# Building the keys of the second head pair on GpSimd, and turning its queries in larger pieces, in an attention and mixture-of-experts kernel

## The chip, the core and the metric

One core of a Trainium2 chip runs the whole program. The metric is device time in microseconds (us): the median of a few executions, each from the first to the last instruction of the program and what lies around it. Smaller is better.

## What is computed

Attention with rotary position codes for 4 batches of 8 heads (576 positions, 64 numbers a head), followed by a mixture of 8 experts in which each token takes one expert:

```python
q_rot, k_rot = rotate(q), rotate(k)                  # x1*cos - x2*sin, x1*sin + x2*cos
attn = softmax(q_rot @ k_rot.T / sqrt(64))
x = attn @ v                                         # heads side by side: 4 x 576 x 512
e = expert_of_token(x)                               # argmax of gates, or the token before's
out = p[e] * (relu(x @ w1[e]) @ w2[e])
```

The output must be as good as fp32. So the kernel splits a number into a rounded part (fp32r, "hi") and the rest ("lo"), and multiplies both.

## The kernel before, in words

**Pairs and steps.** Two heads make a pair; 4 batches of 4 pairs give pairs 0 to 15. A pair takes 9 steps: for each of its two heads four tiles of 128 queries, and one tile that holds the last 64 queries of both heads. So there are 144 steps, and step g belongs to pair g // 9. In each step (the loop from L1270) TensorE computes the scores of the next step (`mm_s`, L255, L273: 4 matmuls of 288 columns; 6 or 10 in a tile of tails), VectorE takes their minimum (L278), ScalarE the exponential (L295), TensorE transposes the result of two steps before (L332), ScalarE rounds that to hi (L310), VectorE subtracts to lo (L314), and from step 11 on TensorE multiplies with the values (L371), five matmuls a step. Up to step 117 the order on every engine is the order of the program. The scores of a step lie in one of two PSUM buffers, so the scores of step g + 2 wait for the exponential of step g.

**What the scores need.** `m` holds a pair's keys: for each head, hi and lo, each on all 128 partitions (the 64 rows twice). `qst` holds its queries, hi in the upper and lo in the lower 64 partitions; `qtail0`/`qtail` hold the tails. There are two buffers for `m` and for `qst`; pair p uses number p % 2.

**Pairs 2 to 15** get them as follows. SyncE (SP) loads q and k in two forms (`load_qk`), GpSimd (POOL) multiplies both with tables of cosines and sines and adds them (`rope_k`, `rope_q`, L200 and L201), splits the sums into hi and lo (`split_qk`, L212 and L213), and SP copies the result to where it is needed with DMAs inside SBUF (`spread`): two for the tails (L240), six for the keys (`spread_k`, L227 to L229) and four for the queries (`spread_q`, L235). A score matmul waits for those copies alone that write what it reads: step 19, the first of pair 2 that is no tile of tails, reads head 0, so it waits for keys' copies one and four and for queries' copies one and three.

**Pairs 0 and 1** are made in another way, in `first_pair` (L1111), so that the work can start early. Their q and k are loaded in a form in which one table multiplication (`products`, L1140; for pair 1 on POOL) leaves two halves that only have to be added, and TensorE adds and duplicates them by a matmul with a 0/1 matrix (`turned`, L1143). ScalarE then rounds the PSUM result to hi (L1152, L1178) and VectorE computes lo (L1155, L1184). Pair 1's keys are made in four pieces of 288 columns (`half_keys`), its queries in four pieces of 256 and 320 columns (`queries`, the second piece of a head with its tail).

**What sets the order around the change.** The dict `START` (L1246) says at the end of which step each of these is issued: pair 1's pieces in steps 3 to 7; `rope_2` and `split_qk(2)`, which make pair 2's queries and keys on POOL, in step 3; `spread(2)` in step 8. POOL and SP work strictly in that order too. On POOL before step 3 stand the four multiplications for pair 1 (L1217) and `split_v(0)` (L218, L219). The loads of the start stand in SP's queue in the order of the program: pair 0's, then pair 1's four (L1201), `wid` (the identity for the transposes, L1229), pair 0's values, a table (L1231), pair 2's, another table, and others.

```python
m_t[1] = m_p.tile([P, 2, 2, S], F32R, tag="m", name="m_1")
pair_1 = [lambda a=a, h=h: half_keys(a, h) for a in range(2) for h in range(2)]
```

## Time and profile before

| | |
|---|---|
| Median of 3 runs | 537.85 us (537.2 to 539.41) |
| The profiled execution's own time | 537.79 us |
| Its span, first to last instruction | 536.0 us |
| TensorE (PE) busy | 515.5 us, 96% of the span |
| VectorE (DVE) busy | 379.1 us, 71% |
| ScalarE (ACT) busy | 344.9 us, 64% |
| GpSimd (POOL) busy | 346.0 us, 65% |
| Mean granted TensorE clock | 0.995 |

Times in the profile count from the start of the span. L12 is line 12 of the kernel. A row of the timeline merges neighbouring instructions of one kind: start, length, engine, line, operation, output<-inputs, count, and in brackets the idle time of the engine before it with what ended that. PEld is TensorE's loading of weights, which runs ahead of the matmuls (PE); DMAs are issued by SP (SPq).

### The profile page before, as it was taken

Reading aid. Unit: us, or ns where it says so; the run is one execution under the profiler, and the core shown is the slowest. Engines: PE = TensorE matmul, PEld = TensorE weight load, DVE = VectorE, ACT = ScalarE, POOL = GpSimd, SP = SyncE. Lnnn points to the kernel's source line nnn. Section 1 sums busy time; section 2 is a strip of 40 time slices with the busy share of each in tenths; the row PEclk is TensorE's granted clock in tenths of the full one; section 3 lists DMA queues with packets and bytes.
Section 4 is the critical chain, followed back from the end, with each engine's and each line's share of the span. In section 5 each row is a group of like instructions: output and inputs, shape, how many; then the busy total and the mean of one; then the engine's idle time right before and its main releaser. Section 6 shows DMA issues by size and latency. Waiting matters only on the chain.

```text
span 536.0 us, 10810 instructions
## 1 busy us (share of the span) xinstructions
PE 515.5 (96%) x3273; PEld 459.1 (86%) x3273; DVE 379.1 (71%) x690; ACT 344.9 (64%) x766; POOL 346.0 (65%) x290
## 2 busy tenths in 40 slices
PE   7999999999999999999999899999999999999992
PEld 4889999999999999998978688887888888888881
DVE  6999999999999999999998746447421745421630
ACT  3988999999999999987866423252433344533440
POOL 4999999999999999795898202355512554411332
PEclk9999999999999999999999999999999999999998
DMA  8758878987889879866168214553637486547340
GB/s 270 285 127 224 229 211 242 239 183 213 226 225 245 206 180 238 228 162 137 24 205 230 66 32 165 169 226 105 191 101 235 141 332 181 172 102 235 98 160 25
DMA packets 65481, 97.33 MB, mean 182 GB/s; under 512 B 28353, under 2 KB 39105, under 8 KB 65282
## 3 DMA queue, kind: packets, MB, share of 16 engines
q1 hardware_dynamic: 61938, 86.45, 57.3%
q0 software_dynamic: 3040, 9.71, 5.8%
q8 instruction: 28, 0.46, 0.4%
q14 instruction: 43, 0.35, 0.2%
q10 hardware_dynamic: 432, 0.36, 0.2%
HBM read 76.95 MB, written 12.86 MB: 168 GB/s over the span
## 4 chain that ended last, share of the span: by engine, by line
PE 80%; DVE 9%; issue 3%; ACT 3%; POOL 2%; DMA 1%; ACTq 0%; POOLq 0%; SPq 0%; DVEq 0%
PE h L981 18%; PE o L1024 17%; PE pv L371 14%; PE s L273 13%; PE tm L332 9%; PE gx L457 3%; DVE mn L278 2%; PE th L1015 2%; DVE ptl L314 2%; PE tx L967 1%; ACT e L295 1%; PE tk L342 1%; DVE w L926 1%; DMA turn<-in_turn_dram 1%; DMA rows_d<-xrow 1%
## 5 line engine op out<-in xcount | busy, mean ns | idle before, releaser
L1024 PE MATMUL o<-w,hs 128*128 128x512 f32 x456 | 113.0, 398 | 0.0
L278 DVE TENSOR_REDUCE mn<-s 128x1 f32<-128x576 f32 x144 | 107.1, 745 | 2.4 <-PE s L273 1.1
L981 PE MATMUL h<-w,xs 128*128 128x512 f32 x444 | 106.1, 392 | 1.2 <-DVE xs L314 0.9
L295 ACT ACTIVATE e<-s,mn 128x576 f32<-128x576 f32 x128 | 95.4, 745 | 16.4 <-DVE mn L278 13.9
L314 DVE TENSOR_TENSOR ptl<-tm,pth 128x512 fp32r<-128x512 f32 x139 | 95.5, 688 | 11.8 <-ACT pth L310 8.8
L1030 POOL DMA_INDIRECT out_dram<-os,sidx x19 | 23.3, 1229 | 124.5 <-ACTq L932 83.0
L273 PE MATMUL s<-m,qst 128*128 128x288 f32 x512 | 96.8, 311 | 4.6 <-ACT e L295 2.7
L981 PEld LDWEIGHTS h<-w,xs 128*128 128x128 f32 x444 | 82.6, 188 | 19.4 <-DVE xs L314 1.4
L1024 PEld LDWEIGHTS o<-w,hs 128*128 128x128 f32 x456 | 83.1, 188 | 17.0 <-DVE hs L314 0.4
L310 ACT CAST pth<-tm 128x512 fp32r<-128x512 f32 x139 | 80.6, 580 | 7.1 <-PE tm L332 6.5
L273 PEld LDWEIGHTS s<-m,qst 128*128 128x128 f32 x512 | 74.1, 188 | 10.1 <-ACT e L295 5.3
L332 PE MATMUL tm<-wid,e 128*128 128x128 f32 x512 | 77.0, 272 | 0.0
L371 PE MATMUL pv<-pth,v 128*128 128x288 f32 x256 | 76.7, 315 | 0.1
L371 PE MATMUL pv<-ptl,v 128*128 128x288 f32 x256 | 76.5, 314 | 0.1
L200 POOL TENSOR_TENSOR stage<-stage 128x1152 f32<-128x1152 f32 x26 | 69.3, 2666 | 0.9 <-DMA stage<-in_qk_dram 0.9
L332 PEld LDWEIGHTS tm<-wid,e 128*128 128x128 f32 x512 | 62.1, 140 | 0.8 <-DVE ptl L314 0.4
L926 DVE TENSOR_TENSOR w<-stage,w 128x1024 fp32r<-128x1024 f32 x37 | 51.2, 1420 | 14.5 <-ACT w L923 9.7
L371 PEld LDWEIGHTS pv<-pth,v 128*128 128x128 f32 x256 | 48.3, 189 | 1.4 <-issue 0.4
L371 PEld LDWEIGHTS pv<-ptl,v 128*128 128x128 f32 x256 | 48.3, 189 | 0.5 <-POOL ptl L307 0.4
L314 DVE TENSOR_TENSOR xs<-tx,xs 128x512 fp32r<-128x512 f32 x19 | 13.1, 688 | 44.1 <-ACTq L932 34.3
L201 POOL TENSOR_TENSOR stage<-stage 128x576 f32<-128x576 f32 x26 | 37.0, 1423 | 2.0
L314 DVE TENSOR_TENSOR hs<-th,hs 128x512 fp32r<-128x512 f32 x26 | 17.5, 687 | 27.4 <-ACTq L932 15.8
(202 smaller groups left out, 822.0 us busy)
## 6 DMA issues: line engine op xcount, KB each, us to landing
stage<-in_wts_dram SPq DMA_DIRECT2D x84, 512.0 KB
stage<-in_qk_dram SPq DMA_DIRECT2D x26, 576.0 KB
qst<-xq SPq DMA_DIRECT2D x56, 128.0 KB
stage<-in_v_dram SPq DMA_DIRECT2D x16, 320.0 KB
m<-xq SPq DMA_DIRECT2D x14, 288.0 KB
m<-xk SPq DMA_DIRECT2D x14, 288.0 KB
m<-xq SPq DMA_DIRECT2D x14, 256.0 KB
m<-xk SPq DMA_DIRECT2D x14, 256.0 KB
```

Source lines behind the costliest of these rows:

```text
L200: engine.tensor_tensor(x, x, tab[:, 2 * f:2 * f + 2], op=ALU.mult)
L201: engine.tensor_tensor(rr[:, f], x[:, 0], x[:, 1], op=ALU.add)
L273: pe.matmul(st[:, h, lo:hi], lhs, keys[:, k0:k0 + hi - lo], start=(n == 0), stop=(n == len(parts_) - 1))
L278: dve.tensor_reduce(mn, s_t[g][:, :, 0:HALF], axis=AX.XY, op=ALU.min)
L295: act.activation(dst.rearrange("p (h s) -> p h s", h=2), s_t.pop(g)[:, :, 0:HALF], AF.Exp, bias=mn, scale=-1.0, accum_out=sums[:, col:col ...
L310: act.copy(hi, src)
L314: dve.tensor_tensor(lo, src, hi.bitcast(F32), op=ALU.subtract)
L332: pe.transpose(ps[:, k], src[:, k * P:(k + 1) * P], ident)
L371: pe.matmul(pv_t[p, u], lhs.rearrange("p c d -> p (c d)"), rhs, start=(n == 0), stop=(n == 9))
L926: (pool if k in on_pool else dve).tensor_tensor(lo, src, hi.bitcast(F32), op=ALU.subtract)
L981: pe.matmul(ps[:, c], xs_t[t][:, x, k], w[y][:, c * 512:(c + 1) * 512], start=(k == 0 and n == 0), stop=(k == 3 and n == 2))
L1024: pe.matmul(ps, hs_t[t][:, x, k], w[y][:, (k % 2) * 512:(k % 2 + 1) * 512], start=(k == 0 and n == 0), stop=(k == 7 and n == 2))
```

## The change

Pair 1's keys are no longer made by TensorE, ScalarE and VectorE. POOL multiplies their two forms by two tables, adds them and splits them into hi and lo, and SP spreads them with the six DMAs of `spread_k(1)`, issued in step 2 ahead of `load_qk(3)`. For this they are loaded in the form of the later pairs, and the fourth table (`tab[:, 3]`) is loaded earlier, between pair 1's second and third load; pair 1's loads come in the order 0, 2, 3, 1. Pair 1's queries are turned in one piece of 512 columns a head (steps 4 and 5), and both heads' tails in a piece of 128 columns (step 7). The function that makes pair 0's remaining keys loses its arguments for pair 1.

```diff
     def split_qk(p):
         parts = [(xq, rr)] if p % 2 == 0 else [(xk[1], rr[:, 1]), (xq[:, :, 0], rr[:, 0])]
         for x, src in parts:
-            pool.tensor_scalar(x[:, 0], src, 1.0, 1.0, op0=ALU.mult, op1=ALU.mult)
-            pool.tensor_tensor(x[:, 1], src, x[:, 0].bitcast(F32), op=ALU.subtract)
+            split_half(x, src)
+
+    def split_half(x, src):
+        pool.tensor_scalar(x[:, 0], src, 1.0, 1.0, op0=ALU.mult, op1=ALU.mult)
+        pool.tensor_tensor(x[:, 1], src, x[:, 0].bitcast(F32), op=ALU.subtract)
...
         dve.memset(raw[:, 0, :, 0:1], 0.0)
-        for x in (2, 3, 0, 1):
+        for x in (0, 2, 3, 1):
+            if x == 3:
+                sp.dma_start(tab[:, 3], tabs[:, 3])
             sp.dma_start(raw[:, 0, x], qk[0, 1, :, x])
...
-        for x in (2, 3, 0, 1):
-            products(x, engine=pool, of=raw[:, 0])
-        m_t[1] = m_p.tile([P, 2, 2, S], F32R, tag="m", name="m_1")
-        pair_1 = [lambda a=a, h=h: half_keys(a, h) for a in range(2) for h in range(2)]
-        pair_1 += [lambda a=a, lo=lo, hi=hi: queries(a, lo, hi, 1)() for a in range(2) for lo, hi in ((0, 256), (256, S))]
+        products(0, engine=pool, of=raw[:, 0])
+        for x in range(2):
+            pool.tensor_tensor(raw[:, 0, 2 + x], raw[:, 0, 2 + x], tab[:, 2 + x], op=ALU.mult)
+        pool.tensor_tensor(rr[:, 1], raw[:, 0, 2], raw[:, 0, 3], op=ALU.add)
+        split_half(xk[1], rr[:, 1])
+        products(1, engine=pool, of=raw[:, 0])
+
+        def queries_1(a):
+            ps = ps_t.tile([P, 512], F32, tag="t", name=f"q1_{a}")
+            turned(a, ps, 0, 512, raw[:, 0])
+            return scaled(qst[1][:, a], ps)
+
+        def tails_1():
+            ps = ps_t.tile([P, 512], F32, tag="t", name="q1_tail")
+            for a in range(2):
+                turned(a, ps[:, 64 * a:64 * a + 64], 512, 64, raw[:, 0])
+            dst = qtail0[1].rearrange("p a (c s) -> p (a c) s", c=2)[:, 0:4:3]
+            return scaled(dst, ps[:, 0:P].rearrange("p (a s) -> p a s", a=2))
+
+        def scaled(dst, src):
+            act.activation(dst, src, AF.Copy, scale=-0.125)
+            low = slice(64, 128)
+            dve.scalar_tensor_tensor(dst[low], src[low], -0.125, dst[low].bitcast(F32), op0=ALU.mult, op1=ALU.subtract)
+
+        pair_1 = [lambda: queries_1(0), lambda: queries_1(1), tails_1]
...
-        sp.dma_start(tab[:, 3], tabs[:, 3])
...
-            0: [lambda: split_v(0)], 1: [rest_q[1], lambda: keep_awake(1)], 2: [rest_q[2], lambda: load_qk(3)],
-            3: [pair_1[0], pair_1[1], rope_2, lambda: split_qk(2)], 4: [pair_1[2]], 5: pair_1[3:5],
-            6: pair_1[5:6], 7: pair_1[6:8] + [lambda: split_v(1), lambda: load_v(2)],
+            0: [lambda: split_v(0)], 1: [rest_q[1], lambda: keep_awake(1)], 2: [rest_q[2], lambda: spread_k(1), lambda: load_qk(3)],
+            3: [rope_2, lambda: split_qk(2)], 4: pair_1[0:1], 5: pair_1[1:2],
+            7: pair_1[2:3] + [lambda: split_v(1), lambda: load_v(2)],
             8: [lambda: spread(2)], 40: [lambda: act.copy(trib, trif)],
```

## Rows read from the trace of the kernel before

**Rows 1.** The chain that ended last, by line: 13 to 30 us, then 44 to 225 us.

```profile
by line: DVE mn L278 29.2%; DVE ptl L314 16.7%; DVE qst L1184 14.6%; issue 10.4%; DVE m L1155 10.0%; ACT e L295 4.9%; DVE qtail L1184 3.4%; PE q L1144 3.2%; ACT pth L310 2.8%; ACT qst L1178 2.3%; ACT pkh L310 1.6%; PE s L273 0.8%; ACT qtail
...
by line: PE pv L371 33.0%; PE s L273 32.3%; PE tm L332 24.0%; PE gx L457 7.3%; PE tk L342 2.7%; PE tt L348 0.7%; issue 0.1%
```

**Rows 2.** Stretches: busy us (and count) of each engine, clock, DMA share, GB/s.

```profile
15.00:20.00 5.00, 4.74 (x33) 4.25 (x33) 4.88 (x10) 4.59 (x13) 4.92 (x4) 1.00 1.01 401
```

**Rows 3.** VectorE to 30 us by shape: count, busy us, mean ns, idle before.

```profile
L314 DVE TENSOR_TENSOR ptl<-tm,pth 128x512 fp32r<-128x512 f32 x8 | 5.5, 689 | 0.2
L1184 DVE SCALAR_TENSOR_TENSOR qst<-q,qst 64x256 fp32r<-64x256 f32 x8 | 3.3, 427 | 0.5 <-ACT qtail L1178 0.3
L1155 DVE TENSOR_TENSOR m<-k,m 128x288 fp32r<-128x288 f32 x6 | 2.5, 450 | 0.0
...
L1184 DVE SCALAR_TENSOR_TENSOR qtail<-q,qtail 64x64 fp32r<-64x64 f32 x4 | 0.9, 222 | 0.0
```

**Rows 4.** Timeline of TensorE: score matmuls of step 10 and loads of steps 19, 28.

```profile
27.31 0.78 PE L273 MATMUL s<-m,qst 128*128 128x288 f32 x4 [0.54 <-DVE qst L1184]
...
43.50 0.56 PEld L273 LDWEIGHTS s<-m,qst 128*128 128x128 f32 x4 [0.35 <-ACT et L295]
...
59.93 0.58 PEld L273 LDWEIGHTS s<-m,qst 128*128 128x128 f32 x4
```

**Rows 5.** Timeline of GpSimd.

```profile
9.20 1.43 POOL L1141 TENSOR_TENSOR raw<-raw,stage 128x576 f32<-128x576 f32 x1
11.10 4.14 POOL L1141 TENSOR_TENSOR raw<-raw,stage 128x576 f32<-128x576 f32 x3 [0.47 <-DMA raw<-in_qk_dram]
...
20.23 1.41 POOL L201 TENSOR_TENSOR stage<-raw 128x576 f32<-128x576 f32 x1
...
27.08 2.68 POOL L213 TENSOR_TENSOR xq<-stage,xq 128x1152 fp32r<-128x1152 f32 x1
...
40.33 0.67 POOL L212 TENSOR_SCALAR xk<-stage 128x576 fp32r<-128x576 f32 x1
41.08 1.45 POOL L213 TENSOR_TENSOR xk<-stage,xk 128x576 fp32r<-128x576 f32 x1
...
225.41 0.28 POOL L470 TENSOR_TENSOR gm<-xrow,sum 128x54 f32<-128x54 f32 x1 [3.41 <-DVE sum L444]
```

**Rows 6.** GpSimd's waits from 60 to 225 us: us, times, longest.

```profile
POOL stage L200 <- DMA stage<-in_qk_dram: 0.9, 1, 0.9
```

**Rows 7.** Timeline of SyncE's queue: the spreads of pair 2 and pair 3's last.

```profile
29.78 1.37 SPq L240 DMA_DIRECT2D qtail<-xq  x2
31.26 0.59 SPq L227 DMA_DIRECT2D m<-xq  x1
...
36.37 3.01 SPq L235 DMA_DIRECT2D qst<-xq  x4
...
52.63 0.83 SPq L229 DMA_DIRECT2D m<-xk  x1
```

**Rows 8.** Stretches, columns as in rows 2: the first loads, and pair 2's spread.

```profile
0.00:9.00 9.00, 7.25 (x23) 3.49 (x23) 5.20 (x19) 2.90 (x5) 1.79 (x6) 1.00 0.75 237
14.00:20.00 6.00, 5.74 (x41) 5.16 (x40) 5.73 (x12) 5.59 (x16) 5.92 (x4) 1.00 1.01 407
...
31.00:40.00 9.00, 9.00 (x70) 8.76 (x71) 8.71 (x16) 8.44 (x21) 8.84 (x5) 1.00 0.79 181
```

**Rows 9.** Timeline of TensorE: the first matmuls, and those after its longest early gap.

```profile
1.19 4.33 PE L1136 MATMUL wake_ps<-wake 128*128 128x512 bf16 x10 [1.19 <-DVE one_c L1188]
...
12.21 0.80 PE L273 MATMUL s<-m,qst 128*128 128x288 f32 x4 [1.19 <-ACT e L295]
```

**Rows 10.** Stretches, columns as in rows 2: after the last matmul.

```profile
528.00:530.00 2.00, 0.00 (x0) 0.00 (x0) 0.00 (x0) 0.00 (x0) 0.10 (x1) 1.00 0.18 60
530.00:532.00 2.00, 0.00 (x0) 0.00 (x0) 0.00 (x0) 0.00 (x0) 0.00 (x0) 0.73 0.00 0
```

More of the change, by code (lines that the diff above doesn't have):

```diff
@@ L1144, in turned, with half_keys @@
             pe.matmul(dst, sel, of[:, x, lo:lo + n], start=True, stop=True)
-        def half_keys(a, h, p=1, wait=False):
-            ps = ps_t.tile([P, 512], F32, tag="t", name=f"k{p}_{a}_{h}")
-            for c, lo, n in (((0, 0, HALF),), ((0, HALF, HALF),), ((64, 0, 224), (0, 512, 64)), ((0, 224, HALF),))[2 * a + h]:
-                turned(2 + a, ps[:, c:c + n], lo, n, raw[:, 0] if p else qkl)
-            hi, lo = (m_t[p][:, a, c, h * HALF:(h + 1) * HALF] for c in range(2))
+        def half_keys(h):
+            ps = ps_t.tile([P, 512], F32, tag="t", name=f"k_1_{h}")
+            for c, lo, n in (((64, 0, 224), (0, 512, 64)), ((0, 224, HALF),))[h]:
+                turned(3, ps[:, c:c + n], lo, n)
+            hi, lo = (m_t[0][:, 1, c, h * HALF:(h + 1) * HALF] for c in range(2))
             act.copy(hi, ps[:, 0:HALF])
@@ L1155, in rest @@
                 dve.tensor_tensor(lo, ps[:, 0:HALF], hi.bitcast(F32), op=ALU.subtract)
-            return rest if wait else rest()
+            return rest
         def keys(a):
@@ L1169, in keys, with queries @@
             return rest
-        def queries(a, lo, hi, p=0):
-            ps = ps_t.tile([P, 512], F32, tag="t", name=f"q{p}_{a}_{lo}")
-            turned(a, ps[:, 0:hi - lo], lo, hi - lo, raw[:, 0] if p else qkl)
+        def queries(a, lo, hi):
+            ps = ps_t.tile([P, 512], F32, tag="t", name=f"q_{a}_{lo}")
+            turned(a, ps[:, 0:hi - lo], lo, hi - lo)
             parts = []
@@ L1176, in queries @@
                 if c1 > c0:
-                    dst, src = qtail0[p][:, a, 64 * a:64 * a + 64] if c0 == 512 else qst[p][:, a, c0:c1], ps[:, c0 - lo:c1 - lo]
+                    dst, src = qtail0[0][:, a, 64 * a:64 * a + 64] if c0 == 512 else qst[0][:, a, c0:c1], ps[:, c0 - lo:c1 - lo]
                     act.activation(dst, src, AF.Copy, scale=-0.125)
@@ L1210, in first_pair @@
         queries(0, 0, 256)()
-        second = [half_keys(1, h, 0, True) for h in range(2)]
+        second = [half_keys(h) for h in range(2)]
         second.append(queries(1, 0, 256))
@@ L1401, in _laid_out, with turned @@
 def _laid_out(q, k, v, moe_w_gate, moe_w_local, moe_w1, moe_w2):
-    def turned(x):
+    def turned(x, own):
         t = x.reshape(B, NP, 2, S, 2, D // 2).transpose(0, 1, 2, 4, 5, 3)
@@ L1405, in turned @@
         x[:, :, 1] = x[:, :, 1, :, ::-1].copy()
-        for hp in range(2):
+        for hp in range(own):
             y = x[0, hp].copy()
@@ L1411, in turned @@
         return x.reshape(B, NP, P, 2, S)
-    qk = np.concatenate([turned(q), turned(k)], axis=3)
+    qk = np.concatenate([turned(q, 2), turned(k, 1)], axis=3)
     vp = v.reshape(B, NP, 2, S, D)
```

## The prediction, made before the changed kernel ran

> **What bounds the kernel now.** I read the chain of waits first, cut in two: from 13 to 30 us it runs over VectorE (its minima, subtractions, and the lo parts of pair 0's and pair 1's queries and keys), from 44 to 225 us over nothing but TensorE [rows 1]. So work taken from VectorE can pay only in the first 30 us, and whatever TensorE has gained or lost when pair 2 begins is carried to the end. Busy time by stretch shows that the front has a second full engine: of 5 us from 15 on VectorE works 4.88 and GpSimd 4.92 [rows 2]. GpSimd's timeline and its waits then show that this isn't a matter of the front alone: between 60 and 225 us it waits once, for 0.9 us [rows 6], and only at 225.41 is it 3.41 us ahead of its work [rows 5]. GpSimd is on no chain, but it has no gap that could take up new work. What it makes is handed on by SyncE's queue, so I read that queue last, and the row in which TensorE first uses pair 2's copies.
>
> **The front.** VectorE loses pair 1's four key pieces, 4 x 0.45 us, and its query pieces, 4 x 0.427 + 2 x 0.222; in all 3.95 us of busy time. It gets two subtractions over 512 columns and one over 128. For the former I take the 0.689 us of the 512-column subtraction from PSUM, for the latter 0.27, between the 64 and the 256 columns [rows 3]. That is 1.65 us, so at most 2.3 us come off. At least nothing does, if ScalarE, which has the casts and exponentials of the same steps, takes over the bound. It is nearly as full as VectorE (4.59 of 5 us in [rows 2]), and loses copies of the same pieces, so I take 1.6. Step 10's scores then start at 25.7 instead of 27.31 [rows 4], and step 19's could start at 43.50 - 1.6 = 41.9. TensorE loses matmuls too, but waits in this stretch, so I cost them at nothing.
>
> **Loads.** One table of 288 KB moves ahead of two of pair 1's loads, of the identity and of pair 0's values. At the 407 GB/s of that time [rows 8] each comes 0.7 us later. The upper bound is 1.4 us, the time from the first use of the fourth place's load that would now be possible (11.10 + 1.38 = 12.48) to the one that is seen to go without a wait (13.86) [rows 5]. I take 0.1 for GpSimd's third multiplication and nothing for the rest, whose first users come later.
>
> **GpSimd.** The four multiplications stay, two with other tables. New are an addition over 576 columns, 1.41 us, and a split, 0.67 + 1.45 us; all three have their like in pairs 2 and 3 [rows 5]. They stand ahead of pair 1's last multiplication, of the split of pair 0's values, and of everything that makes pair 2. With the 0.1 from above, all of that comes 3.6 us later, since there is no gap before. The values of pair 0 aren't needed until the first product in step 11, some 10 us later; nothing there.
>
> **Pair 1's keys.** GpSimd ends them at 11.10 + 0.1 + 3 x 1.4 + 0.67 + 1.45 = 17.5. SyncE then issues six copies, ahead of pair 3's load, which isn't used before step 9. The copies are 1.18 MB; at the 181 GB/s of pair 2's spread [rows 8], begun 1.2 us after the first issue as there (29.78 to 31.0) [rows 7, 8], they have moved by 25.2. Step 9 needs two of the first four, step 10 the last. That is 0.5 us before step 10 could start (25.7): hidden, with little to spare. Even a delay would cost nothing by itself until 28.3, as the next part shows.
>
> **Pair 2's queries decide.** SyncE starts pair 2's spread at 29.78, when GpSimd ends the split (27.08 + 2.68) [rows 5, 7]. Step 19 needs the third of the four query copies. Up to its end the spread moves 64 + 1152 + 3 x 128 = 1600 KB, 1.64 MB; 9 us at 181 GB/s from 31 on make 1.63 MB [rows 8]. So its last byte goes at 40.05. What passes until TensorE may use it isn't shown. It is at least nothing. At most it is the 2.1 us that pair 1's second load needed: the 2.13 MB up to its end had moved by 9.0 (237 GB/s) [rows 8], and GpSimd waited for it until 11.10 [rows 5]. I take one issue interval, 3.01 / 4 = 0.75 us [rows 7], so 40.8, nearer to the low end, since these copies go out one after another with little else beside them. Before, step 19 started at 43.50 and waited for ScalarE, not for a copy [rows 4]: 2.7 us to spare. With 3.6 us more the copy is there at 44.4. TensorE, ready at 41.9, waits 2.5 us, the whole gain of the front goes, and another 0.9 with it. With both ends of the lag step 19 starts between 43.65 and 45.75, +0.15 to +2.25.
>
> **Behind that.** Pair 3's last key copy is issued by 53.46 [rows 7] and used at 59.93 or later [rows 4]: 6.5 us to spare against 3.6 - 0.9 = 2.7, so nothing. The later pairs follow the same pattern, and GpSimd catches up where it now idles 3.41 us. From 44 on the chain is TensorE's, so +0.9 stands at the end: 537.79 + 0.9 = 538.7 for the profiled execution. That execution lies 0.06 below the median of the runs shown, so I leave the number as it is.
>
> **Rivals.**
>
> *The copies end with their issue.* If the transfers aren't what takes the time, the third query copy ends when its issue does, at 36.37 + 3 x 0.75 = 38.6; 3.6 later that is 42.2, step 19 starts 1.3 us earlier than before, and the end is 536.5. The issues of the spread are wide apart for a queue that only feeds (3.01 us for four), which speaks for it. Against it speaks that the copies' bytes last until 40.05, 1.4 us beyond. Chance 0.17. The Trainium skill has a rule that points this way: in "DMA: Bandwidth & Descriptors", "Why small descriptors are slow (HBM only)" exempts copies within SBUF from the price of small pieces, and "Where 436 GB/s comes from" bounds them by the fabric's 435 GB/s; an estimate by it is 4 us for the 1.77 MB of a spread. The trace disagrees: 181 GB/s with the engines 0.79 busy, beside 407 GB/s for loads [rows 8].
>
> *The clock falls in the new wait* (slower). Place: the 2.5 us without a matmul before step 19. At the start ten matmuls of 512 columns take 4.33 us, 0.43 each, which is the level of 1.2 GHz (the clock column reads 1.00 there, so I go by the duration) [rows 8, 9]. If the wait put TensorE there for as long, 4.3 us of it would do half the work: +2.2, 540.9. It decides once a gap is long enough. After 1.19 us without work the matmuls ran as ever [rows 9], and a stretch of 2 us after the last matmul still reads 1.00 before the next falls to 0.73 [rows 10]. 2.5 us lies little above that; chance 0.08. The Trainium skill, "TensorE: Matmul & The Clock Gate", section "HAM oscillation", tells of such waits for DMA between groups of matmuls that let the clock fall.
>
> *Pair 1's keys are late.* If their copies share the engines with the loads that run until 20 and beyond [rows 8], add up to 3 us: 28.2, plus a lag of 0.75 to 2.1, up to 30.3, which is 3.0 behind step 10 of before. The likely cost is half, 539.3, as loads issued earlier go first and then end. Chance 0.08.
>
> If ScalarE holds the front, so that nothing is gained there, the end is 538.7 all the same: step 19 waits for GpSimd's work, not for the front.
>
> **The numbers.** The forecast has 0.67. A half per cent (2.7 us) is about what a measurement of this kernel can tell from no change. No case reaches 535.1: even the whole 2.3 us of the front gives 535.5; faster 0.04. Slower than 540.5 are the clock's case and the upper tail of the keys' and of the lag: 0.12. The same: 0.84. The range reaches from the first rival, 536.2 with a little more gain, to the upper lag with a late load, 540.3, and leaves the clock out.
>
> **What would show it.** Right: step 10's scores about 1.6 us earlier than 27.31; GpSimd's split of pair 2 ending near 33.4; the first spread of pair 2 issued there; TensorE idle some 2.5 us before the scores of step 19, released by a copy into `qst`, at about 44.4; afterwards every row 0.9 later than before. Wrong: step 19 released by ScalarE as before (then the copies had more room than I read), a wait before steps 9 or 10 (the keys), matmuls at twice their length behind the wait (the clock), or a copy of pair 3 or later that ends a wait.

## The result and the profile after

The kernel with the change takes 540.86 us (median of 6, 539.75 to 542.39), the kernel before, run beside it, 537.3 (median of 6). The ratio is 1.0067, 95% interval 1.005 to 1.0083: slower by 3.6 us, where the prediction had 0.9 and a range up to 540.3. The profiled execution took 541.03 us with a span of 538.8; against the one before that is 3.24 us, 2.8 of them within the span.

GpSimd's timeline after the change, to be held against [rows 5]: the addition and the split at 14.09 to 17.8 are new, and pair 2's split ends at 33.71 for 29.76, 3.95 us later.

```profile
11.10 2.92 POOL L1223 TENSOR_TENSOR raw<-raw,stage 128x576 f32<-128x576 f32 x2 [0.33 <-DMA raw<-in_qk_dram]
14.09 1.41 POOL L1224 TENSOR_TENSOR stage<-raw 128x576 f32<-128x576 f32 x1
15.59 0.68 POOL L215 TENSOR_SCALAR xk<-stage 128x576 fp32r<-128x576 f32 x1
16.35 1.42 POOL L216 TENSOR_TENSOR xk<-stage,xk 128x576 fp32r<-128x576 f32 x1
17.74 1.41 POOL L1144 TENSOR_TENSOR raw<-raw,stage 128x576 f32<-128x576 f32 x1
...
31.01 2.70 POOL L216 TENSOR_TENSOR xq<-stage,xq 128x1152 fp32r<-128x1152 f32 x1
```

SyncE's queue after the change: pair 1's copies from 17.80, pair 2's from 33.73, its queries from 40.17 (36.37 in [rows 7]).

```profile
17.80 0.55 SPq L230 DMA_DIRECT2D m<-xk  x1
...
21.70 0.85 SPq L232 DMA_DIRECT2D m<-xk  x1
...
33.73 1.25 SPq L243 DMA_DIRECT2D qtail<-xq  x2
...
40.17 3.05 SPq L238 DMA_DIRECT2D qst<-xq  x4
```

TensorE's timeline after the change: the scores of steps 9 and 10, then of step 19, what follows it, and step 20.

```profile
25.60 0.77 PE L276 MATMUL s<-m,qst 128*128 128x288 f32 x4 [1.33 <-ACT et L298]
26.71 0.77 PE L276 MATMUL s<-m,qst 128*128 128x288 f32 x4
...
44.80 1.12 PE L276 MATMUL s<-m,qst 128*128 128x288 f32 x4 [2.56 <-DMA qst<-xq]
45.72 1.05 PE L335 MATMUL tm<-wid,e 128*128 128x128 f32 x4
...
47.24 0.44 PE L374 MATMUL pv<-ptl,v 128*128 128x288 f32 x1
47.48 0.44 PE L374 MATMUL pv<-pth,v 128*128 128x288 f32 x1
...
48.20 0.81 PE L276 MATMUL s<-m,qst 128*128 128x288 f32 x4
```

Step 19 waits 2.56 us for a query copy, as forecast, and then comes what was not: the work behind the wait takes nearly twice its time. From step 19 to step 20 it is 3.40 us; in the kernel before it is 1.96:

```profile
43.50 0.80 PE L273 MATMUL s<-m,qst 128*128 128x288 f32 x4
...
45.46 0.69 PE L273 MATMUL s<-m,qst 128*128 128x288 f32 x4
```

The stretches of the change tell why (columns as in [rows 2]; the clock is the column ahead of the last two):

```profile
44.00:44.50 0.50, 0.00 (x0) 0.00 (x0) 0.00 (x0) 0.00 (x0) 0.50 (x2) 1.00 0.95 205
44.50:45.00 0.50, 0.20 (x1) 0.23 (x2) 0.00 (x0) 0.00 (x0) 0.42 (x1) 1.00 1.27 183
45.00:46.00 1.00, 1.00 (x6) 0.98 (x6) 0.04 (x1) 0.00 (x0) 0.99 (x1) 0.51 0.79 276
46.00:48.00 2.00, 2.00 (x11) 2.00 (x10) 1.28 (x2) 1.19 (x3) 1.92 (x3) 0.50 1.01 401
48.00:48.50 0.50, 0.50 (x4) 0.50 (x4) 0.46 (x2) 0.47 (x3) 0.50 (x1) 0.57 0.98 384
48.50:50.00 1.50, 1.50 (x14) 1.50 (x14) 0.76 (x1) 0.64 (x2) 1.50 (x2) 1.00 0.32 117
```

TensorE works through 45 to 48 without a gap, at 1.2 GHz in place of 2.4; in all the clock stands low for 3.4 us, from 45.0 to 48.4. One more wait stands on VectorE in step 38, of a kind that the kernel before doesn't have:

```profile
82.47 0.42 DVE L474 TENSOR_TENSOR xrow<-gx,sum 128x256 f32<-128x256 f32 x1 [0.39 <-DMA rows_d<-xrow]
```

For all kernels of this study (the experiments follow below) the table gives how much later than in the kernel before a step's minimum starts on VectorE, in us, worked out from the traces step by step, one execution of each kernel; negative is earlier. The last column is the difference of the spans.

```
step                    8     12     18     19     20     27     36     45     90    126    143   span
before, at us        25.2   32.7   43.1   44.7   46.3   59.5   75.9   92.3  174.4  241.4  279.2  536.0
the change          -1.23  -1.15  -1.14  +1.30  +2.72  +2.85  +2.86  +3.09  +3.11  +3.05  +3.04   +2.8
e3 queries only     +0.28  -0.34  -0.33  -0.34  -0.34  -0.33  -0.35  -0.34  -0.34  -0.34  -0.37   +0.5
e4 keys only        -1.16  -0.89  -0.86  +0.88  +1.20  +1.19  +1.17  +1.87  +1.86  +1.80  +1.78   +1.2
e2 before, GpSimd late
                    -0.08  -0.08  -0.07  +1.19  +1.51  +1.51  +1.51  +2.04  +2.01  +1.95  +1.90   +1.7
e7 the same, later  -0.92  -0.92  -0.90  +2.92  +4.69  +5.23  +5.21  +5.26  +5.22  +5.15  +5.13   +3.9
e1 filler of 20     -1.01  -1.42  -1.39  +2.38  +2.70  +2.69  +2.70  +2.74  +2.81  +2.77  +2.77   +3.4
e6 filler of 10     -0.78  +1.02  +1.05  +3.03  +3.35  +3.33  +3.33  +3.34  +3.38  +3.31  +3.30   +3.7
e8 add on VectorE   -0.02  -0.69  -0.65  +0.73  +1.85  +2.40  +2.40  +2.97  +2.91  +2.90  +2.89   +2.5
e10 off GpSimd      +3.74  +3.06  +3.08  +3.08  +3.08  +3.08  +3.08  +3.12  +3.15  +3.12  +3.08   +1.8
e11 the same        +3.73  +3.05  +3.08  +3.07  +3.08  +3.05  +3.07  +3.11  +3.12  +3.09  +3.07   +3.5
e5 head 0 first     -0.87  -1.54  -1.54  -1.54  -1.53  -1.15  +0.52  +2.49  +2.53  +2.56  +2.55   +2.2
e9 and the add      -0.02  -0.69  -0.67  -0.67  -0.67  -0.67  -0.67  +1.80  +1.73  +1.74  +1.75   +1.6
e12 all pairs so    -1.04  -1.70  -1.68  -1.69  -1.68  -1.37  -1.37  +5.56  +5.72  +5.72  +5.74   +5.1
e13 stores ahead    -1.31  -1.67  -1.65  -1.66  -1.66  -1.18  -1.20  -1.21  -1.25  -1.23  +6.65   +6.7
e14 before, so      -0.20  -0.21  -0.21  -0.21  -0.22  -0.21  -0.21  -0.18  -0.25  -0.20  +7.81   +7.2
e15 to pair 8       -1.18  -1.50  -1.46  -1.46  -1.46  -1.31  -1.06  -0.77  -0.27  +3.14  +3.15   +3.1
e16 before, so      -0.69  -0.70  -0.67  -0.68  -0.68  -0.70  -0.46  -0.19  +0.31  +3.59  +3.54   +2.8
```

So the change is 1.15 us early at step 18, loses 2.44 in the wait, 1.42 in the slow stretch, 0.13 in the step behind it and 0.24 at step 38, and keeps the rest to the end of attention. The experts' part varies by more than half a us between the profiled executions: e10 and e11 end attention alike and their spans differ by 1.8.

Not all of the 1.15 us is the change's doing. No computing engine does anything different ahead of step 0's minimum, and yet it starts 0.38 us earlier in the change's execution than in the one before; over all kernels it lies between 0.92 earlier (e7) and 0.34 later (e10), and among kernels with the change's own order of loads between 0.72 earlier (e13) and those 0.34 later. It moves with the landing of the first loads. The first keys of pair 0, in the kernel before and in the change:

```profile
6.08 1.21 PE L1144 MATMUL k<-stage,turn 128*128 128x288 f32 x4 [0.56 <-DMA turn<-in_turn_dram]
```

```profile
5.69 1.21 PE L1147 MATMUL k<-stage,turn 128*128 128x288 f32 x4 [0.77 <-DMA turn<-in_turn_dram]
```

So the change's own share at step 18 is some 0.77 us, and an entry of the table under about a us says little of a kernel by itself; what changes along a row is sounder. A second point on reading it: where step 19 waited and the clock stayed (e1, e2, e4, e6), its minimum followed its scores 0.3 us sooner than in the kernel before. The 0.32 between the columns 19 and 20 of these rows is therefore no loss.

### The profile page after: what moved, and what is told of

Read it like the earlier page. It is cut to its first block, busy times and chain, and to the rows that moved or that the text cites. A ratio compares the mean times of both kernels' runs of the same rounds, so it can differ in the third digit from the quotient of the medians.

```text
span 538.8 us, 10789 instructions
## 1 busy us (share of the span) xinstructions
PE 515.1 (96%) x3263; PEld 458.3 (85%) x3263; DVE 377.9 (70%) x683; ACT 343.6 (64%) x759; POOL 349.7 (65%) x293
```

## The experiments

Theory at first: the wait that GpSimd's lateness makes, plus the lower clock behind it, are the loss. Rivals: the copies of pair 1's keys; the queries' new pieces; something later.

### The change taken apart

**e3**: the kernel before, with the change's queries alone.

```diff
-        pair_1 += [lambda a=a, lo=lo, hi=hi: queries(a, lo, hi, 1)() for a in range(2) for lo, hi in ((0, 256), (256, S))]
...
+        pair_1 += [lambda: queries_1(0), lambda: queries_1(1), tails_1]
...
```

> The kernel before with the queries' half of the change alone: pair 1's queries in pieces of 512 columns, both tails in one; keys as before. Theory: VectorE saves 0.5 us of busy time, step 10 starts up to 0.5 us earlier, GpSimd isn't late, step 19 waits for no copy and the clock stays: 0 to -0.5, 537.0. Rival A: TensorE does about as much as before here, so it expects no fall either.

Measured: 538.22 us, ratio 1.0006 (0.9993 to 1.0019, 12 runs): no difference. From step 12 on every step of the attention is 0.34 us earlier (0.10 of it at step 0 already), and no copy is waited for. This half is sound and nearly worth nothing.

**e4**: the change, with the queries in the four pieces of before.

```diff
-        pair_1 = [lambda: queries_1(0), lambda: queries_1(1), tails_1]
...
+        pair_1 = [lambda a=a, lo=lo, hi=hi: pieces_1(a, lo, hi) for a in range(2) for lo, hi in ((0, 256), (256, S))]
...
```

> The changed kernel with pair 1's queries in the four pieces of the kernel before: the keys' half alone. Theory: GpSimd is as late as in the changed kernel, so step 19 starts at 44.8 again; the front is some 0.4 us slower, so the gap is about 2.1 us instead of 2.56 and lies between the 1.2 us that left the clock alone and the 2.56 us that did not: 538.7 if it stays, 540.5 if it falls. Rival A: more matmuls in the front than in the changed kernel, so the clock rather stays.

Measured: 541.29 us, ratio 1.0067 (1.0053 to 1.0082), the whole loss. In the profiled execution, its fastest (539.5), the wait is 2.19 us and the clock stays at 1.00; VectorE's wait of step 38 is 0.83 us, and 0.7 more is lost there. Its other executions have a mean clock of 0.991 to 0.995, so some of them may hold the slow stretch; but the kernel before's own executions reach from 0.992 to 0.996, and e4's longest (542.16) has 0.995. What makes them up to 2.7 us longer than the profiled one is open.

**e2**: the kernel before, with an addition and a split on GpSimd behind pair 1's multiplications, whose results nothing reads. No copy and no load of the change.

```diff
             products(x, engine=pool, of=raw[:, 0])
+        pool.tensor_tensor(rr[:, 1], raw[:, 0, 2], raw[:, 0, 3], op=ALU.add)
+        pool.tensor_scalar(xk[1][:, 0], rr[:, 1], 1.0, 1.0, op0=ALU.mult, op1=ALU.mult)
+        pool.tensor_tensor(xk[1][:, 1], rr[:, 1], xk[1][:, 0].bitcast(F32), op=ALU.subtract)
```

> The kernel before with the changed kernel's addition and split added on GpSimd behind pair 1's products; their results are used by nothing, so nothing but GpSimd's lateness is new (some 3.6 us). Theory: step 19's scores wait for a copy into qst until about 44.5, 1.0 us later than the kernel before's 43.50; the gap in TensorE is about 1.4 us, too short for the clock; the end is +1.0, 538.3. Rival B (the late copies come from SyncE's longer queue and the traffic of pair 1's copies, not from GpSimd): no wait at step 19, time within 0.3 of the kernel before.

Measured: 540.3 us, ratio 1.0047 (1.003 to 1.0065), 2.6 us above the kernel before and so more than the 1.0 expected; the profiled execution, 539.7, is among its faster ones. GpSimd's lateness alone makes the wait ahead of step 19, and 0.53 us more at step 38:

```profile
45.04 0.77 PE L273 MATMUL s<-m,qst 128*128 128x288 f32 x4 [1.73 <-DMA qst<-xq]
```

So the wait and most of the loss need nothing of the keys' copies or loads; they follow from 3.5 us of work on GpSimd.

### The clock

**e1**: the change, with 20 matmuls that nothing reads ahead of step 19's scores.

```diff
+        def fill(n=20):
+            ps = ps_t.tile([P, 512], F32, tag="t", name="fill")
+            for _ in range(n):
+                pe.matmul(ps[:, 0:P], ident, ident, start=True, stop=True)
...
-            8: [lambda: spread(2)], 40:
+            8: [lambda: spread(2)], 17: [fill], 40:
```

> The changed kernel with 20 matmuls of the identity with itself, results unused, at the end of step 17, so that TensorE works in the 2.56 us in which step 19's scores wait for the queries' copies. Theory (GpSimd is 3.9 us late, so the copies are late, and the wait itself lets TensorE's clock fall): step 19 starts at 44.8 as in the changed kernel, the clock column stays at 1.00 behind it, step 20 comes 2.0 us later instead of 3.4, and the end is 1.4 us earlier than the changed kernel's, 539.4. Rival A (the clock falls because TensorE has less to do in the front since the keys left it): the clock falls all the same, time within 0.4 of 540.9.

Measured: 542.14 us, ratio 1.0077 (1.0059 to 1.0094). The filler took 4.63 us, twice what was meant, and made step 19 itself 1.4 us later than in the change. But the clock stayed at 1.00, step 20 followed 1.94 us after step 19, and it stood where it stands in the change:

```profile
46.21 0.78 PE L276 MATMUL s<-m,qst 128*128 128x288 f32 x4
...
48.15 0.70 PE L276 MATMUL s<-m,qst 128*128 128x288 f32 x4
```

In this execution TensorE, kept at work where the change has its gap, didn't lose its clock; the slow stretch of the change therefore costs about the 1.4 us by which the filler overshot. The end, 542.14, is not the 539.4 expected, since the filler gave away what it saved.

The mean granted clock of all executions, profiled or not, speaks for a fall that isn't of one execution alone: 0.9943 before (17 executions, run beside e1 to e4), 0.9915 with the change (6), 0.9930 in e1 (6), 0.9945 in e2 (6), 0.9892 in e7 below (6). A slow stretch of 3.4 us takes 0.0032 off the mean of 538.8 us. So on average an execution of the change holds nearly one such stretch more than one of the kernel before, one of e1 0.4 and one of e2 none.

**e6**: the same with `n=10`.

> The changed kernel with 10 matmuls ahead of step 19's scores, half as many as in the run with 20, whose result nothing reads: some 2.3 us from about 41.8, so that they end before the copies land. The clock's share by itself. If the 2.56 us gap costs its own length and, through the lower clock, some 1.4 us more: step 19 stays at 44.8 (44.7 to 45.0), the clock column stays 1.00 from 44 to 50, step 20 follows after some 1.95 us (3.40 in the changed kernel), and step 20 is late by some 1.4 us against the kernel before, not 2.7. Of these 1.4 us some 0.5 come back at step 38, where DVE's wait for rows_d grows to some 0.7; end about 539.8. Rival (the lower clock costs nothing, the matmuls behind the gap wait for ScalarE and DVE anyway): step 20 at 48.0 as it was and an end of 540.9.

Measured: 540.62 us, ratio 1.0048 (1.0028 to 1.0068), some 0.2 us by the medians below the change's, which the intervals don't separate. The profiled execution, its slowest, can't answer the question: in it pair 1's key copies came late, step 9 waited 1.47 us for them, and the clock fell behind that wait already, at 28.05.

```profile
26.64 0.77 PE L276 MATMUL s<-m,qst 128*128 128x288 f32 x4 [1.47 <-DMA m<-xk]
```

```profile
28.00:29.00 1.00, 1.00 (x6) 0.98 (x6) 0.70 (x2) 1.00 (x3) 1.00 (x1) 0.53 1.01 410
29.00:30.00 1.00, 1.00 (x7) 1.00 (x5) 0.85 (x2) 0.36 (x3) 0.92 (x2) 0.50 1.00 400
```

So the new wait at step 9 is a second place where the change can lose its clock. At step 19 the clock stayed at 1.00 and step 20 followed 1.92 us behind; but TensorE came there 2.2 us later than in the change and GpSimd's split of pair 2 only 1.1 (to 34.78), so that by estimate some 1.4 us of gap were left to fill. So this execution says little of the filler.

**e7**: e2 with one addition more.

```diff
+        pool.tensor_tensor(rr[:, 0], raw[:, 0, 2], raw[:, 0, 3], op=ALU.add)
```

> The kernel before with two unused adds and the unused split on GpSimd, one add (1.41 us) more than in the run with one. Nothing else of the change is in it. If the length of the gap ahead of step 19 decides over the clock, and nothing of the change's own parts: wait for the copies 1.73 + 1.41 = 3.1 us, the clock column falls to about 0.5 for some 3 us behind it (with one add it stayed 1.00), step 20 late by 1.5 + 1.4 + 1.4 = 4.3 us; end about 542. Rival (the clock fell because of the change's own order of work around the gap): clock 1.00, step 20 late by 2.9, end about 541.

Measured: 542.57 us, ratio 1.0105 (1.0081 to 1.0129). The wait is 3.75 us, the clock falls while it lasts and stays at 1.2 GHz for 6.8 us, to 52.3; step 20 is 4.69 us late, not 2.9.

```profile
46.24 1.30 PE L273 MATMUL s<-m,qst 128*128 128x288 f32 x4 [3.75 <-DMA qst<-xq]
```

```profile
44.00:46.00 2.00, 0.00 (x0) 0.00 (x0) 0.00 (x0) 0.00 (x0) 1.92 (x3) 0.87 0.91 185
46.00:48.00 2.00, 1.76 (x8) 1.78 (x9) 0.43 (x1) 0.00 (x0) 1.92 (x3) 0.50 0.93 378
```

The clock's fall needs nothing of the change's own code either, only the gap.

### Taking work off GpSimd

**e8**: the change, with the addition moved to VectorE in step 0.

```diff
-        pool.tensor_tensor(rr[:, 1], raw[:, 0, 2], raw[:, 0, 3], op=ALU.add)
-        split_half(xk[1], rr[:, 1])
-        products(1, engine=pool, of=raw[:, 0])
+        def sum_k():
+            dve.tensor_tensor(rr[:, 1], raw[:, 0, 2], raw[:, 0, 3], op=ALU.add)
+            split_half(xk[1], rr[:, 1])
+            products(1, engine=pool, of=raw[:, 0])
...
-            0: [lambda: split_v(0)], ...
+            0: [pair_1[3], lambda: split_v(0)], ...
```

The list `pair_1` gets `sum_k` as its last entry.

> The changed kernel with one instruction moved: the add of the second pair's key halves (1.41 us on GpSimd) is made by DVE in step 0, some 0.7 us there. If GpSimd's lateness sets the wait ahead of step 19 and the later one at step 38: GpSimd's end of the third pair's split about 1.4 us sooner (32.3 for 33.7), the copy wait 2.56 - 1.4 = 1.2 us, clock 1.00, shift of about 0 at step 20; behind step 38 the keys-only run's +1.87 less 1.4, some +0.5; end about 538.3. Rival (the copies' own issue and bytes set the wait): wait 2.2 to 2.6 and the time 540.5 to 541. Another (DVE's 0.7 us stands in step 0's chain): all steps from 1 on late by up to 0.7, end about 539.

Measured: 540.5 us, ratio 1.0043 (1.0027 to 1.0059). GpSimd's split of pair 2 starts 2.65 us late and not 3.93, about as expected; the wait is 1.83 us, not 1.2, since from the split's end to step 19 it took 12.2 us here and 11.1 in the change (e2 11.9, e4 11.2): the copies' time varies by a us from execution to execution. And the clock fell to 0.50 from 45.9 to 49.3, which I had excluded. Together with e2 (1.73 us, no fall) and e4 (2.19, none) this says that a gap of some 2 us may or may not bring the clock down; its length alone doesn't decide.

**e10** and **e11**: all three instructions off GpSimd (addition and subtraction on VectorE in steps 1 and 2, rounding on ScalarE); e11 on the change as it is, e10 with the copies of e5 below.

```diff
-        pool.tensor_tensor(rr[:, 1], raw[:, 0, 2], raw[:, 0, 3], op=ALU.add)
-        split_half(xk[1], rr[:, 1])
...
+        def sum_k():
+            dve.tensor_tensor(rr[:, 1], raw[:, 0, 2], raw[:, 0, 3], op=ALU.add)
+            act.copy(xk[1][:, 0], rr[:, 1])
+        def low_1():
+            dve.tensor_tensor(xk[1][:, 1], rr[:, 1], xk[1][:, 0].bitcast(F32), op=ALU.subtract)
...
```

> The changed kernel with the same three instructions off GpSimd and the copies in the change's own order. If GpSimd alone made both the wait ahead of step 19 and the end: its split late by under 0.6 us, the copies land some 3.4 us sooner, the 2.56 us wait is gone, clock 1.00 from 44 to 50, and the shift of step 18 (about -0.9, held at steps 9 and 10 by the keys' copies) stays to the end of attention; end 536.8 to 537.5. Rival (the copies of the second pair's keys, 0.36 MB that the kernel before did not move, are what costs): wait still over 1 us and an end over 538.5.

> The head-first kernel with all three new GpSimd instructions of the keys elsewhere: add and subtraction by DVE (0.76 us each, steps 1 and 2), rounding by ScalarE (0.65). GpSimd then has the kernel before's work but for product order, so its split of the third pair is late by 0.1 to 0.6 and by -0.8 to -0.3 after its one wait. If GpSimd's chain sets the end of attention: shift at step 45 and behind of -1.5 to -1.0 (what the front allows, DVE's 1.5 us included, may make it -0.7); no copy wait at step 19, clock 1.00; end 536.5 to 537.2, below the kernel before by 0.1 to 0.25%. Rival (DVE and ScalarE have no room there and the front gives back all): shift of 0 at step 18 and an end of 538.

Measured: e11 541.06 us, ratio 1.0057 (1.0036 to 1.0077); e10 540.78, 1.0064 (1.0043 to 1.0085). With GpSimd late by 1.28 us only, the wait ahead of step 19 and the slow stretch behind it are gone in both, whatever the order of the copies. But these two runs don't clear the keys' copies (1.18 MB, not the 0.36 of e11's expectation), as they were meant to: all of attention is 3.1 us late there, which is enough to hide a wait of 2.56 us even with GpSimd late as before. As far as the wait ahead of step 19 goes, e2 clears them: it has the wait and none of these copies. The front was late by 4.6 us at step 4: ScalarE stood 2.2 us (e11) behind VectorE's addition, and VectorE's operations took far longer beside a working GpSimd than I had priced them (0.76 us). From e11:

```profile
14.39 1.56 DVE L1227 TENSOR_TENSOR stage<-raw 128x576 f32<-128x576 f32 x1
...
19.23 2.14 DVE L1231 TENSOR_TENSOR xk<-stage,xk 128x576 fp32r<-128x576 f32 x1
```

The rival of e10 (the front gives back all) came nearer, and was still 3 us too low.

In e11's front TensorE stood without a matmul for 2.50 us, and the clock fell there too, for 3.4 us from 18.8:

```profile
17.44 0.80 PE L276 MATMUL s<-m,qst 128*128 128x288 f32 x4 [2.50 <-ACT e L298]
```

```profile
20.00:21.80 1.80, 1.80 (x8) 1.47 (x7) 1.77 (x2) 0.00 (x0) 1.01 (x2) 0.50 0.00 0
```

That cost nothing: in e10, whose clock stayed at 1.00 behind waits of 1.84 and 1.81 us, steps 4 to 18 come at the same times within 0.02 us. VectorE works 1.77 of these 1.80 us. So the slow stretch had no price here, where TensorE was not what the others waited for.

### Where the rest of the lateness goes

GpSimd stays 3.9 us late up to pair 4, then 3.0 to the end of attention (its one wait of [rows 6] is used up). Does that bound the attention by itself, or does it reach TensorE by certain ways only?

**e5**: the change, with the copies of pairs 1 and 2 issued head 0 first and pair 2's first four tiles taken head 0 first, so that step 19 needs half of the copies.

```diff
...
+    def spread_by_head(p):
+        if p > 1:
+            spread_tail(p)
+        m_t[p] = m_p.tile([P, 2, 2, S], F32R, tag="m", name=f"m_{p}")
+        for a in range(2):
+            for c in range(2):
+                keys_of(p, a, c)
+            if p > 1:
+                for c in range(2):
+                    queries_of(p, a, c)
...
-        return (i // 2, i % 2) if p == 0 and i < 4 else (i % 2, i // 2)
+        return (i // 2, i % 2) if p in (0, 2) and i < 4 else (i % 2, i // 2)
...
```

> The changed kernel; the copies of the second and third pairs' keys and queries are issued head 0 first, and the third pair's first four tiles are taken head 0 first, so that step 19 needs 6 of 12 copies and no longer all. GpSimd's lateness stays. If the order of the copies is what makes lateness a wait: steps 9 and 10 no longer held, so shift of about -1.5 us from step 11 to 18; wait ahead of step 19 under 0.6 us and the clock 1.00; shift of -1.5 to -0.5 at step 20. At step 38 GpSimd's lateness still comes back through SP's queue and the rows_d store (the keys-only run stood at +1.87 behind it): wait of 2 us or more for rows_d, shift of +1.3 to +1.9 behind it, end about 539.3. Rival (a store that is only a little late is absorbed, and what was gained ahead stays): shift of -1 behind step 39 too, end about 536.8.

Measured: 540.77 us, ratio 1.0061 (1.004 to 1.0081). Up to step 20 all as expected: 1.54 us early, no wait at step 19, the clock at 1.00. Behind that 4 us are lost, more than I expected, by two ways. Pair 3's scores wait (1.4 us, put down to ScalarE), and at step 38 VectorE waits for a store:

```profile
81.86 0.43 DVE L498 TENSOR_TENSOR xrow<-gx,sum 128x256 f32<-128x256 f32 x1 [2.10 <-DMA rows_d<-xrow]
```

The buffer that VectorE wants is read by a store that stands behind the next pair's spread in SyncE's queue. The kernel before issues that spread at 59.21 and the store at 70.01, this one at 63.30 and 74.00:

```profile
63.30 1.25 SPq L243 DMA_DIRECT2D qtail<-xq  x2
...
74.00 0.38 SPq L508 DMA_DIRECT2D rows_d<-xrow  x1
```

**e9**: e5 with the addition on VectorE in step 1.

> The head-first kernel with the add of the second pair's keys (1.41 us on GpSimd) made by DVE in step 1, where GpSimd's products have ended. Theory now: GpSimd waits once between 20 and 225 us, so what it is given at the start it never gives back, but for that wait of 0.9; TensorE may run ahead of it by some 0.7 us and no more. So with GpSimd's split of the third pair late by 4.05 - 1.4 = 2.65 us (32.4) and later by 1.7, the steps are early by 1 to 1.5 us up to step 20 and late by 1.0 (0.7 to 1.3) from step 45 on, whatever the copies and the clock do; end about 539 (539.0 to 539.5 by the median, ratio 1.002). Rival (the order of the copies takes back what the wait cost, and GpSimd's lateness is only another way to that wait): shift of -1 at step 45 too and an end of 537.

Measured: 539.99 us, ratio 1.0053 (1.0031 to 1.0074). GpSimd was not relieved: I had left the split directly behind the addition, so it stood idle for 1.74 us until VectorE had made it, and stayed 4.06 late. The shift at step 45, +1.80, is again the store (2.6 us of wait), with no wait for copies left.

**e12**: e5 with every later pair's copies and first four tiles head 0 first. **e13**: e12, with the stores of VectorE's rows issued ahead of the next spread. **e14**: e13's two orders in the kernel before. In e12 the lines from `if soon:` to `soon.pop(0)()` are missing.

```diff
...
-                    spread_tail(p + 1)
-                    spread_q(p + 1)
-                    spread_k(p + 1)
+                    if soon:
+                        first_out.append(g)
+                        soon.pop(0)()
+                    spread_by_head(p + 1)
...
```

> The head-first kernel with the copies of all later pairs issued head 0 first and their first four tiles taken head 0 first. In the head-first run two waits took the gain back: one ahead of the fourth pair's tiles (steps 27 and 28) and DVE's 2.1 us for rows_d at step 38. If these are separate doors through which GpSimd's lateness reaches TensorE: the first is gone (shift of -1.5 to -1.1 up to step 36), the second grows to 2.5 to 3.5 us and the shift behind step 39 is +1.3 to +2.5 as it was; end 539.5 to 540.5. Rival (the order of the copies was the only door): shift of -1 behind step 39 and an end of 537.

> The kernel with every pair's copies and tiles head 0 first, and the two stores of DVE's rows (0.1 MB) issued ahead of the next pair's copies on SP's queue, no longer behind them. GpSimd is as late as in the change (+3.9, then +3.0). If copies and stores behind one another on SP are the only ways in which GpSimd's lateness reaches TensorE: no wait over 0.5 us in the attention, clock 1.00, shift of -1.5 to -0.8 from step 11 to the end of attention; end 536.6 to 537.4, below the kernel before by 0.1 to 0.25%. Rival (GpSimd's chain itself is the bound, and another of its results is late next: the split of v, the gates' rows): shift of +1 to +2.5 from some step between 40 and 70 on, end 539.5 to 540.5.

> The kernel before with the same two orders (copies and tiles head 0 first from the third pair on, DVE's rows stored ahead of the copies), nothing of the change. If the orders only take away waits that GpSimd's lateness makes, they give nothing where GpSimd is not late: 537.5 to 538.5, ratio 0.999 to 1.001. Rival (the orders gain by themselves, and a gain of the run beside it is theirs): below 537.2.

Measured: e12 544.18 us, ratio 1.0128 (1.01 to 1.0156): with the copies out of the way the store's wait grew to 4.9 us, more than expected, and the clock fell behind it (0.69 for 80 to 90), where TensorE had stood for 3.55 us. e13 544.83 us, 1.0133 (1.0106 to 1.016), and the answer is in its steps: **1.2 us early at every step from 27 to 126, with GpSimd 4.2 us late throughout**, and no wait of TensorE over 0.93 us from 12 to 200 us. So GpSimd's chain isn't a bound by itself. The total is worthless all the same: behind step 117 a planner lays out the order, and it now put pair 13's values ahead of pair 14's split on GpSimd, where they wait for a buffer:

```profile
227.06 0.73 POOL L227 TENSOR_SCALAR v<-stage 128x640 fp32r<-128x640 f32 x1 [4.71 <-PE pv L404]
```

TensorE then waits for pair 14's queries, and the clock falls in that wait and stands at 0.50 from 243.6 to 253.8. Together this is the jump of 7.9 us behind step 126:

```profile
244.87 1.30 PE L306 MATMUL s<-m,qst 128*128 128x288 f32 x4 [4.44 <-DMA qst<-xq]
```

In e14, 546.21 us (1.0174, 1.0143 to 1.0206), the same happens without the change, and up to step 126 the two orders are worth nothing there. GpSimd is 4.1 us late from 88 us on in e14 as well, by waits that the orders bring with them, and TensorE is as early as it was at step 0: a second execution in which that lateness reaches nothing.

**e15**: e13's order of tiles and of stores up to pair 8 only, which leaves the planner's order as it was (the copies stay head 0 first up to pair 13), and the gates' rows of pairs 0 to 3 on VectorE. **e16**: the same in the kernel before.

```diff
...
-            if j0 == 0 and p < POOL_ROWS:
+            if j0 == 0 and p < POOL_ROWS and p not in (0, 1, 2, 3):
...
+                    if soon and p < 9:
+                        first_out.append(g)
+                        soon.pop(0)()
+                    spread_by_head(p + 1)
...
```

> The head-first kernel with both orders of the run before it (head 0 first, DVE's rows stored ahead of the copies) up to the ninth pair only, so that the planner's part behind step 117 keeps the change's order on TensorE and GpSimd; and the gates' rows of the first four pairs made by DVE, which takes 4 x 1.12 us from GpSimd between 65 and 125 us. If GpSimd's lateness (4 us) reaches TensorE only through the copies and the stores: shift of -1.5 to -0.8 up to step 36 and, GpSimd being on time again by the ninth pair, -1.2 to 0 to the end of attention (DVE's rows are 0.8 us each on an engine that is busy nine tenths there); end 536.5 to 538.0. Rival (GpSimd's chain is a bound by itself): shift of +1 or more behind step 45, end over 539.

> The kernel before with the same orders and the same rows on DVE, nothing of the change: what these are worth by themselves. There are no waits for copies or stores to take away, and TensorE does the same work: shift of 0 to +0.8 (DVE's rows), end 537.5 to 538.5. The difference to the run beside it, 1.0 to 1.5 us expected, is what the change gives where GpSimd's lateness is kept from TensorE. Rival (the orders gain by themselves): below 537.

Measured: e15 541.0 us, ratio 1.0066 (1.0044 to 1.0088); e16 542.09, 1.0083 (1.0058 to 1.0108). The rows cost VectorE 1.1 us over the four pairs in both. GpSimd did not catch up, since with the queries' copies last its own buffer `xq` comes free late (5.6 us of waits for `qst<-xq` up to 160 us in e15, 8.5 in e16); where the old order of tiles and stores starts again, 3.4 us are lost, a store's wait of 2.4 us on VectorE among them. e16 loses 3.3 us at the same place with a store's wait of 1.8, so that loss is made by the mixture of orders and says nothing against the change.

What the change is worth where nothing of it waits can be read from the two pairs of runs. At step 90 e15 is 0.58 us ahead of e16, and at step 126 e13 is 1.0 ahead of e14, of which 0.52 were there at step 0. That makes some 0.5 us, a tenth of a per cent, and the times of e15 and e16, whose intervals overlap, can't show it. A version that beats both kernels was not found. e3 is the one part that costs nothing.

## Why the prediction was wrong

**Where the time went.** Against the profiled execution of before: step 19 is 1.30 us late by its start (forecast 0.9), the slow clock behind it adds 1.42 and 0.13 in the step after, step 38 adds 0.24, the experts' part takes back 0.3, and 0.44 lie outside the span: 3.24 us in all.

**The step that failed** is the rival of the clock: "2.5 us lies little above that; chance 0.08", and a range that "leaves the clock out". The wait was forecast to 0.06 us, and the clock fell 0.2 us behind just that wait. The Trainium skill, "TensorE: Matmul & The Clock Gate", section "HAM oscillation", which the prediction named, describes this kind of event, a wait for DMA between groups of matmuls that start again at half speed; the trace agrees (0.50 from 45 to 48). The waits of that page's example are longer than the 2.56 us here; that this one was enough the trace alone shows. The rows behind the 0.08 were a gap of 1.19 us without harm and a column that still read 1.00 some 2 us after the last matmul [rows 9, 10]; they bound only gaps shorter than the one forecast, so they were no reason against a fall at 2.5. The price was too high: I took 4.3 us at half speed, and it was 3.4, 3.2 of them ahead of step 20, which cost 1.42 us and not 2.2. With 0.9 and 1.4 the sum would have been 540.1; the wait's own 0.4 and the parts below make the rest. That the rival's 540.9 comes so near to the 541.03 is luck: its price was 0.8 too high, and what it left out fills that.

**The front.** Forecast 1.6, got 1.15, of which 0.38 were there at step 0, so 0.77. With the copies head 0 first it is 1.5, counted in the same way (1.54 less 0.02 in e5, 1.68 less 0.20 in e12): the term of VectorE was right. The difference is the step "pair 1's keys: hidden, with little to spare": step 9 waited 1.33 us to 25.60 and step 10 started at 26.71, not 25.7. The profile puts that wait down to ScalarE; it is gone in e5, where only the order of the copies differs up to there, and in e6 it is put down to the copies. The margin of 0.5 us was smaller than the error of an estimate from a mean rate. As said there, that delay cost nothing by itself, for step 19 waited anyway; it made room for a second fall of the clock (e6).

**Loads.** That the moved table costs the loads behind it nothing held in the profiled execution of the change, but was near its edge too. In e6, e13 and e15, whose step 0 comes 0.65 to 0.72 us earlier than in the kernel before, TensorE waits for the identity `wid` at the transposes of step 0 (0.62 us to 14.26 in e6, 0.16 and 0.23 in the others). In e7 and e16, as early but with the old order of the loads, it doesn't.

**GpSimd.** Forecast 3.6 late, measured 3.95. The three instructions take 3.51 us as priced; three hand-offs of 0.08 us between instructions that depend on one another and 0.19 us more for pair 1's split-up multiplications (2.92 + 1.41 for 4.14) make the rest. e2 shows that such lateness (3.37 us there) alone makes the wait.

**Pair 2's queries decide.** Right in mechanism and nearly in size: idle 2.56 us for 2.5, step 19 at 44.80 for 44.4, 3.95 - 3.6 = 0.35 of that from GpSimd. Part of the match is luck: TensorE, forecast to be ready at 41.9, was ready at 42.25, so both ends of the wait came 0.4 later. The copies' rate came out as read from [rows 8]: the rival that they end with their issue, 536.5, did not happen.

**"Behind that ... nothing"** failed too. I followed pair 3's copies (6.5 us to spare) and not the other work that stands behind a spread in SyncE's queue. The store of VectorE's rows does, and its buffer is wanted at step 38. In the change 2.85 us of lateness on TensorE hide most of it, 0.24 us remain; where TensorE is less late it takes 0.5 to 0.7 (e2, e4), and where TensorE isn't late 2 to 5 us (e5, e9, e12). So even without the clock's fall the end would hardly have been as early as +0.9: e4's execution without one ends attention at +1.8.

**Open.** The 0.44 us outside the span. It is nearly the same in every execution of a kernel, within 0.25, but not from kernel to kernel (1.8 us before and in e3, 1.9 in e5, 2.0 in e2, 2.2 to 2.3 in the change, e1, e4 and e6, and 1.8 again in e12, e13 and e15, which hold the change); no run isolates what makes it. Open is also what, besides its length, lets a gap of about 2 us bring the clock down.

## What to carry to other kernels

An engine that is on no chain but has no gap is a debt without repayment: what is given to it at the start is late to the end, so list everything that its lateness can reach, the work that stands behind its copies in a queue included, and not only the copies themselves. A wait that a change opens on TensorE has to be priced with its length and with a stretch at half speed behind it as soon as it is longer than the gaps that the trace shows to be harmless. And a copy that is hidden by half a microsecond on paper is not hidden.

## What the runs showed of the hardware

- The granted clock fell from 2.4 to 1.2 GHz in or behind waits of TensorE of 1.47 us (e6, at step 9), 1.83 (e8), 2.50 (e11, in the front), 2.56 (the change), 3.55 (e12), 3.75 (e7), 4.01 (e14) and 4.44 (e13). It did not behind 1.33 us (the change, at step 9), 1.42 (e5), 1.73 (e2), 1.81 and 1.84 (e10) or 2.19 (e4). Among waits of 1.4 to 2.2 us both happened. In the longest ones (e7, e13, e14) it fell while TensorE still waited, in the others 0.2 to 1.4 us after the next matmuls had begun. In the change it came back after 3.4 us in which TensorE worked without a gap.
- VectorE's two-operand instruction over 128x576 numbers in SBUF takes 0.76 us while GpSimd waits (e9), and 1.56 and 2.14 us (e11) while GpSimd works on SBUF operands of its own. GpSimd's rounding of pair 0's values, 0.72 us in the change, took 1.23 us then:

```profile
15.31 1.23 POOL L221 TENSOR_SCALAR v<-stage 128x640 fp32r<-128x640 f32 x1
```

The Trainium skill, "SBUF — State Buffer", section "Who interferes with whom", has this rule: an instruction of VectorE with two inputs in SBUF contends with a GpSimd instruction that reads SBUF, and one with at most one such input doesn't. e11 agrees, and so does the change, where VectorE's subtractions from PSUM keep their 0.69 us beside a full GpSimd. Had I gone by it, the expectations of e10 and e11 would have been slower than before.
